# Attention, layer norm and feed-forward on one core: first scores of the next batch, two-part statistics, the last pair's normalisation, the low part of q, and the order of the weight conversions

## The chip, the core and the metric

The kernel runs on one core of a Trainium2 chip. The metric is the device time of one execution in microseconds (us). Five engines work from queues of their own, each in program order: TensorE (PE: matmuls and transposes; PEld: its weight loads), VectorE (DVE), ScalarE (ACT), GpSimd (POOL) and SyncE (SP, which issues the transfers here). A semaphore wait at the head of a queue holds up all that stands behind it.

## The reference

Causal attention over 4 batches, 12 heads, 448 positions and 64 columns a head, in float32; then a layer norm over the 768 columns, a two-layer feed-forward and a residual.

```python
scores = scale * np.matmul(q, k.transpose(0, 1, 3, 2))
scores = np.where(mask, -1000000000.0, scores)
attn = np.exp(scores - np.max(scores, axis=-1, keepdims=True))
attn = attn / (np.sum(attn, axis=-1, keepdims=True) + 1e-09)
x = np.matmul(attn, v)          # heads side by side: (4, 448, 768)
xn = (x - mu) / np.sqrt(var + 1e-06) * g_ln
out = x + np.maximum(xn @ w_ch1, 0.0) @ w_ch2     # 768 -> 3072 -> 768
```

The feed-forward weights come as 64-bit numbers, which the kernel turns into float32 itself.

## The kernel before

**Feed-forward.** All of it is paced by slots, 48 for each batch. A slot is 18 matmuls of 128x448: each float32 operand is a high part and a low part, and high x high, high x low and low x high are added in PSUM. Slots 0 to 11 and 24 to 35 are the first layer (`ph`, L421), the others the second (`po`, L440). `xh`/`xl` are the parts of the normalised input, `hh`/`hl` those of the hidden layer (eviction of `ph` by ACT at L426, then DVE at L427), `wh`/`wl` those of a slot's weights. In batch 0 a slot's weights are converted from the raw 64-bit numbers, four slots ahead: two ACT passes (`convert1`: `w` and `bits`), one on DVE (`convert2`), then ACT writes `wh` (`split1`) and DVE `wl` (`split2`). Later batches read float32 copies back (`full`) and only split them.

**Attention.** Heads go in six pairs (p = 0 to 5) a batch. For a pair: the score matmuls in five groups of row blocks (`SGROUPS`), a DVE pass over each block that masks and finds the row's extreme (L242), the exponential on ACT (`exps`, L256), the division by the row sums (`norm`, L272, on DVE; in batch 0 on POOL for p below `NDVE`), transposes in five groups (`pt`, L288) copied to SBUF as `PT` (L291 on ACT, L293 on DVE), and the product with v (`px`, L303), which ACT copies to `xT` (L307). Batch 0 multiplies in float32. From batch 1 on q and k are split first: ACT writes q's high part `qs`, DVE k's high part `kh`, DVE the low part of q into the other 64 partitions of `qs` (L200), POOL the low part of k, `kl` (L203).

**Layer norm.** `stats` transposes `xT` back (`pln`, L316), up to three column blocks of 128 at a time, and DVE takes the statistics of the piece (`bn_stats`, L319); `aggr` joins them (L326), POOL raises to the power -1/2 (L328), `spread` (PE) puts mean (`mb`) and factor (`rb`) on all partitions, and DVE (`xg`), ACT (`xh`) and POOL (`xl`, L361) write the six blocks.

**Order.** The program is written slot by slot: first what `pre` holds (loads, splits of q and k, exponentials, normalisations, the apply steps of the layer norm), then the weight steps (`ahead`), then the slot's matmuls with their evictions, then `post` (scores, transposes, products with v, statistics). Batch 0's attention lies in the slots below zero, the prologue, with batch 1's first pair begun there; batch b + 1's attention is woven into the feed-forward of batch b, a pair every six slots. PSUM buffers: `sc` 2, `mm` 3 (for `ph`, `po` and in the prologue some scores), `pt` 2 (for transposes and `pln`), `pv` 1 (`px`).

## Time and profile before

| | us |
|---|---|
| three runs | 918.36, 919.53, 921.22 (median 919.53) |
| the profiled execution | 919.61 |
| its span, first to last instruction | 917.8 |
| PE busy in the span | 897.9 (98%) |
| DVE, ACT, POOL busy | 553.8, 452.8, 121.8 |
| mean granted TensorE clock | 0.992 |
| prologue, up to the first feed-forward matmul | 80.04 |
| feed-forward of batches 0, 1, 2, 3 | 221.90, 218.38, 218.41, 179.07 |

What lies around the span is 1.81 us. A timeline row gives start, duration, engine, line, operation, output<-input, shapes and a count; in brackets stands how long the engine stood idle before it and whose end it waited for. A row with a count above 1 joins neighbours of one kind. A row of stretches gives the stretch, its length and then each engine's busy time with its instruction count, the granted clock, the share of the DMA engines and the bytes moved. A matmul's duration includes its pass through the array, so neighbours overlap: the pace is the distance of their starts.

### The profile page before, as it was taken

How to read it: one execution, taken by the hardware profiler on the slowest of the kernel's cores; microseconds unless marked ns; L12 is line 12 of the kernel's file. 1: busy time of each engine (PE TensorE's matmuls, PEld its weight loads, DVE VectorE, ACT ScalarE, POOL GpSimd, SP SyncE). 2: the span in 40 equal slices, each digit the busy share in tenths (PEclk: the TensorE clock that was granted, in tenths of full speed). 3: DMA queues.
4: the chain of work that ended last, by engine and by line, in shares of the span. 5: the costliest groups of instructions: out<-in, count | busy, mean ns of one | idle time of the engine just before them, and what ended most of it. 6: DMA issues, size and time to landing. Idle time of an engine off the chain costs nothing.

```text
span 917.8 us, 12820 instructions
## 1 busy us (share of the span) xinstructions
PE 897.9 (98%) x4864; PEld 790.2 (86%) x4864; DVE 553.8 (60%) x1208; ACT 452.8 (49%) x907; POOL 121.8 (13%) x115
## 2 busy tenths in 40 slices
PE   6988999999999999999999999999999999999998
PEld 4656889888899988988889998888988999999997
DVE  4877788777778566655664676556664634333431
ACT  5955888778865544444442355433542333222320
POOL 5543111101021111100102210011100200000000
PEclk9998999999999999999999999999999999999999
DMA  9920778787778643333313634343222343323210
GB/s 245 338 76 22 287 260 281 282 305 248 254 258 272 232 154 110 109 123 119 103 48 123 214 126 151 120 152 111 84 96 77 120 148 116 120 104 104 103 65 31
DMA packets 35246, 144.36 MB, mean 157 GB/s; under 512 B 4080, under 2 KB 8688, under 8 KB 35184
## 3 DMA queue, kind: packets, MB, share of 16 engines
q1 hardware_dynamic: 35184, 143.54, 45.2%
q8 instruction: 38, 0.62, 0.3%
q14 instruction: 24, 0.20, 0.1%
HBM read 119.15 MB, written 24.38 MB: 156 GB/s over the span
## 4 chain that ended last, share of the span: by engine, by line
PE 88%; ACT 5%; DVE 4%; DMA 1%; issue 1%; SPq 1%; POOL 0%; ACTq 0%
PE po L440 38%; PE ph L421 34%; PE px L303 5%; PE sc L234 4%; PE pt L288 4%; ACT P L256 2%; PE pln L316 1%; DMA raw<-w_dram 1%; PE sc L227 1%; ACT w L99 1%; ACT bits L103 1%; ACT wh L122 1%; DVE P L272 1%; DVE hl L427 1%; DVE wl L126 1%
## 5 line engine op out<-in xcount | busy, mean ns | idle before, releaser
L421 PE MATMUL ph<-xh,wh 128*128 128x448 f32 x576 | 214.5, 372 | 1.4 <-ACT xh L358 1.4
L440 PE MATMUL po<-hh,wh 128*128 128x448 f32 x576 | 214.1, 372 | 0.0
L421 PE MATMUL ph<-xl,wh 128*128 128x448 f32 x576 | 211.7, 368 | 0.5 <-POOL xl L361 0.5
L421 PE MATMUL ph<-xh,wl 128*128 128x448 f32 x576 | 211.3, 367 | 0.2
L440 PE MATMUL po<-hh,wl 128*128 128x448 f32 x576 | 210.7, 366 | 0.0
L440 PE MATMUL po<-hl,wh 128*128 128x448 f32 x576 | 210.6, 366 | 0.0
L427 DVE SCALAR_TENSOR_TENSOR hl<-ph,hh 128x448 fp32r<-128x448 f32 x96 | 59.8, 624 | 145.6 <-ACT hh L426 145.6
L122 ACT ACTIVATE wh<-full 128x768 fp32r<-128x768 f32 x144 | 119.3, 838 | 53.7 <-PE po L440 50.8
L126 DVE TENSOR_TENSOR wl<-full,wh 128x768 fp32r<-128x768 f32 x144 | 136.4, 953 | 0.8 <-ACT wh L122 0.5
L426 ACT ACTIVATE hh<-ph 128x448 fp32r<-128x448 f32 x96 | 52.0, 543 | 153.4 <-PE ph L421 153.2
L256 ACT ACTIVATE P<-P,nm 112x448 f32<-112x448 f32 (+3 forms) x176 | 91.7, 523 | 68.0 <-DVE nm L242 68.0
L421 PEld LDWEIGHTS ph<-xh,wl 128*128 128x128 f32 x576 | 108.6, 189 | 10.6 <-DVE wl L126 2.2
L421 PEld LDWEIGHTS ph<-xh,wh 128*128 128x128 f32 x576 | 108.7, 189 | 10.3 <-ACT xh L358 1.7
L421 PEld LDWEIGHTS ph<-xl,wh 128*128 128x128 f32 x576 | 108.7, 189 | 8.9 <-POOL xl L361 1.0
L440 PEld LDWEIGHTS po<-hh,wl 128*128 128x128 f32 x576 | 108.1, 188 | 9.2 <-DVE wl L126 0.4
L440 PEld LDWEIGHTS po<-hh,wh 128*128 128x128 f32 x576 | 108.2, 188 | 8.5
L440 PEld LDWEIGHTS po<-hl,wh 128*128 128x128 f32 x576 | 108.4, 188 | 8.2
L242 DVE CUSTOM_DVE_ANT_0 P<-sc,mask 112x448 f32<-112x448 f32 (+3 forms) x176 | 70.6, 444 | 51.9 <-PE sc L234 39.6
L203 POOL TENSOR_TENSOR kl<-qkraw,kh 128x896 fp32r<-128x896 f32 x18 | 51.8, 2878 | 377.0 <-DVE kh L193 370.3
L444 DVE TENSOR_TENSOR xT<-po,xT 128x448 f32<-128x448 f32 x48 | 29.9, 623 | 112.7 <-PE po L440 112.7
L288 PE MATMUL pt<-ident,P 112*112 112x112 f32 x440 | 55.1, 262 | 3.8 <-ACT PT L291 2.6
L288 PEld LDWEIGHTS pt<-ident,P 112*112 112x112 f32 x440 | 46.9, 134 | 13.5 <-ACT PT L291 4.1
(63 smaller groups left out, 941.8 us busy)
## 6 DMA issues: line engine op xcount, KB each, us to landing
full<-scratch SPq DMA_DIRECT2D x72, 768.0 KB, 4.2
raw<-w_dram SPq DMA_DIRECT2D x48, 768.0 KB, 5.7
scratch<-w SPq DMA_DIRECT2D x48, 384.0 KB, 2.9
qkraw<-qk_dram SPq DMA_DIRECT2D x18, 896.0 KB, 7.5
out_dram<-xT SPq DMA_DIRECT2D x24, 224.0 KB, 2.0
vt<-v_dram SPq DMA_DIRECT2D x18, 224.0 KB, 5.4
first_qk<-qk_dram SPq DMA_DIRECT2D x8, 224.0 KB, 5.5
rest<-v_dram SPq DMA_DIRECT2D x6, 224.0 KB, 7.8
```

The costliest lines, as they stand in the source:

```text
L122: nc.scalar.activation(out=wh[s], in_=w32[s], func=ACTF.Copy)
L126: nc.vector.tensor_tensor(out=wl[s], in0=w32[s], in1=wh[s].bitcast(F32), op=ALU.subtract)
L203: nc.gpsimd.tensor_tensor(out=kl, in0=rk, in1=kh.bitcast(F32), op=ALU.subtract)
L234: nc.tensor.matmul(pt[:, o:o + n], lhsT=qs[:, h, C * i:C * i + C], rhs=kk[:, h, :n], start=(part == 0), stop=(part == 1),)
L242: nc.vector.tensor_tensor_reduce(out=self.t["P", p, h][:, OFF[i]:OFF[i + 1]], in0=pt[:, o:o + n], in1=mask[:, S - n:], op0=ALU.add, op1=AL ...
L256: nc.scalar.activation(out=pp, in_=pp, func=ACTF.Exp, scale=-1.0, bias=nm[:, x:x + 1], accum_out=self.t["sm", p, h][:, i:i + 1],)
L288: nc.tensor.transpose(pt[:, o:o + C], pp[:, a:a + C], ident[:C, :C])
L303: nc.tensor.matmul(px[D * h:D * h + D, C * j:], lhsT=vt[:, h, j, :], rhs=self.t.pop(("PT", p, h, j)), start=(j == 0), stop=(j == NC - 1),)
L421: nc.tensor.matmul(pm[y], lhsT=w[:, c * P:c * P + P], rhs=z[:, c, :], start=(c == 0 and i == 0), stop=(c == KC - 1 and i == 2),)
L426: nc.scalar.activation(out=hh[:, x + y, :], in_=pm[y], func=ACTF.Relu)
L427: nc.vector.scalar_tensor_tensor(out=hl[:, x + y, :], in0=pm[y], scalar=0.0, in1=hh[:, x + y, :].bitcast(F32), op0=ALU.max, op1=ALU.subtract,)
L440: nc.tensor.matmul(pm, lhsT=w[:, o:o + P], rhs=z[:, x, :], start=(x == 0 and i == 0), stop=(x == HF - 1 and i == 2),)
```

## The change

- **Batch 1's first pair.** Its five score groups stood in the prologue ahead of the products of batch 0's last pair. Now the products of groups 0 and 1 stand behind the last statistics, in `mm` buffers, with their DVE pass (`lows`) behind `aggr` and their exponentials between the `xh` blocks; groups 2 and 3 come after the first feed-forward slot, group 4 after the second. The splits of its q and k come later too (`PARTS`), and all of batch 1's later steps one slot later, its transposes two.
- **Statistics of batch 0** are taken in two parts of three column blocks, not in three of 3, 2 and 1, and the first part starts two slots earlier.
- **`NDVE` 7 to 5:** batch 0's last pair is normalised on DVE.
- **Low part of q** (18 instructions, 64x896): from DVE to POOL, ahead of `kl`.
- **`convert1`** in slots from 0 on is queued behind the slot's evictions and `post` steps, not ahead of them.

```diff
--- before.py
+++ after.py
@@ -29,17 +29,19 @@
 
 SGROUPS = [[(0, 3)], [(0, 0), (0, 2)], [(0, 1), (1, 1)], [(1, 3)], [(1, 0), (1, 2)]]
 TGROUPS = [[(0, 0)], [(0, 1), (0, 3)], [(0, 2), (1, 2)], [(1, 0)], [(1, 1), (1, 3)]]
-HOLE = [-7, 1]
+HOLE = 2
+AHEAD = [-205, -204, -203, -200, -200, -199]
 EARLY = 45
 GAP = 6
 FIRST = -20
+PARTS = [-18, -13]
 SAT0, TAT0, NAT0, END0, EV0 = [-1, 0, 2, 2, 4], [7, 8, 9, 10, 11], [4, 6], 13, [1, 1, 0, 1, 0]
 SAT, TAT, NAT, END, EV = [0, 0, 1, 1, 2], [3, 4, 4, 5, 5], [3, 4], 6, [1, 1, 0, 0, 0]
-EV1 = [1, 1, 1, 1, 1]
-TH0, TH = [38, 40], [18, 30]
+TAT1, END1, EV1 = [4, 5, 5, 6, 6], 7, [1, 1, 1, 1, 1]
+TH0, TH1, TH = [36], [20, 32], [18, 30]
 ELAG = [2, 5, 7]
-NDVE = 7
-STATS = [(0, 3), (3, 5), (5, 6)]
+NDVE = 5
+STATS0, STATS = [(0, 3), (3, 6)], [(0, 3), (3, 5), (5, 6)]
 LAST = 239 / 256
 OFF = [C * (i * (i + 1) // 2) for i in range(NC + 1)]
 
@@ -157,6 +159,7 @@
     class Att:
         def __init__(self, b):
             self.b = b
+            self.spans = STATS if b else STATS0
             self.t = {}
             self.turn = 0
             self.done = set()
@@ -197,19 +200,25 @@
             r = self.t.pop(("raw", p))
             qs, kh, kl = self.t["qk", p]
             rq, rk = r[:, 0:2, :], r[:, 2:4, :]
-            nc.vector.tensor_tensor(
+            nc.gpsimd.tensor_tensor(
                 out=qs[D:], in0=rq[D:], in1=qs[D:].bitcast(F32), op=ALU.subtract
             )
             nc.gpsimd.tensor_tensor(out=kl, in0=rk, in1=kh.bitcast(F32), op=ALU.subtract)
 
         def scores(self, p, grp):
+            self.products(p, grp)
+            self.lows(p, grp)
+
+        def products(self, p, grp):
             if self.b == 0:
                 tag, bufs = (("sc", 2), ("sc", 2), ("mm", 3), ("mm", 3), ("mm", 3))[self.turn % 5]
                 self.turn += 1
+            elif self.b == 1 and p == 0 and grp in SGROUPS[:2]:
+                tag, bufs = "mm", 3
             else:
                 tag, bufs = "sc", 2
             pt = ps.tile([C, S], F32, tag=tag, name="sc", bufs=bufs)
-            nm = sb.tile([C, 2], F32, tag="nm", name="nm", bufs=8)
+            self.t["sc", p, tuple(grp)] = pt
             o = 0
             for h, i in grp:
                 n = C * (i + 1)
@@ -236,6 +245,10 @@
                             start=(part == 0), stop=(part == 1),
                         )
                 o += n
+
+        def lows(self, p, grp):
+            pt = self.t.pop(("sc", p, tuple(grp)))
+            nm = sb.tile([C, 2], F32, tag="nm", name="nm", bufs=8)
             o = 0
             for x, (h, i) in enumerate(grp):
                 n = C * (i + 1)
@@ -308,7 +321,7 @@
             self.done.add(("pv", p))
 
         def stats(self, part, x):
-            c0, c1 = STATS[part]
+            c0, c1 = self.spans[part]
             assert all(("pv", c) in self.done for c in range(c0, c1))
             self.done.add(("stats", part, x))
             pt = ps.tile([C, S], F32, tag="pt", name="pln")
@@ -321,9 +334,10 @@
         def aggr(self):
             mv = sb.tile([C, NC, 2], F32, tag="mv", name="mv", bufs=2)
             ve = sb.tile([C, NC], F32, tag="ve", name="ve", bufs=2)
-            assert all(("stats", i, x) in self.done for i in range(3) for x in range(NC))
+            n = len(self.spans)
+            assert all(("stats", i, x) in self.done for i in range(n) for x in range(NC))
             for x in range(NC):
-                nc.vector.bn_aggr(out=mv[:, x, :], in_=self.stat[:, x])
+                nc.vector.bn_aggr(out=mv[:, x, :], in_=self.stat[:, x, :n])
             nc.vector.tensor_scalar_add(ve, mv[:, :, 1], 1e-6)
             nc.gpsimd.tensor_tensor(out=ve, in0=ve, in1=mhalf, op=ALU.pow)
             self.t["mv"], self.t["ve"] = mv, ve
@@ -374,7 +388,9 @@
             if self.b == 0:
                 sat, tat, nat, end, ev = SAT0, TAT0, NAT0, END0, EV0
             else:
-                sat, tat, nat, end, ev = SAT, TAT, NAT, END, EV1 if self.b == 1 else EV
+                sat, tat, nat, end, ev = SAT, TAT, NAT, END, EV
+            if self.b == 1:
+                tat, end, ev = TAT1, END1, EV1
             period = 6
             for p in range(NP):
                 t0 = period * p
@@ -388,14 +404,24 @@
                 for x, grp in enumerate(TGROUPS):
                     put(post, t0 + tat[x], self.transposes, p, grp, "act" if ev[x] else "dve")
                 for x, grp in enumerate(SGROUPS):
+                    if self.b == 1 and p == 0:
+                        if x < 2:
+                            put(post, AHEAD[0], self.products, p, grp)
+                            put(post, AHEAD[1], self.lows, p, grp)
+                            put(pre, AHEAD[2], self.exps, p, grp)
+                        else:
+                            put(post, AHEAD[x + 1], self.scores, p, grp)
+                            put(pre, AHEAD[x + 1] + 1, self.exps, p, grp)
+                        continue
                     put(post, t0 + sat[x], self.scores, p, grp)
                     put(pre, t0 + sat[x] + 1, self.exps, p, grp)
             tl = period * (NP - 1) + end + 1
-            th = TH0 if self.b == 0 else TH
+            th = TH0 if self.b == 0 else TH1 if self.b == 1 else TH
             for x in range(NC):
                 put(post, th[0] + x, self.stats, 0, x)
-                put(post, th[1] + x, self.stats, 1, x)
-                put(post, tl + x // 2, self.stats, 2, x)
+                if self.b:
+                    put(post, th[1] + x, self.stats, 1, x)
+                put(post, tl + x // 2, self.stats, len(self.spans) - 1, x)
             ta = tl + NC // 2
             put(pre, ta, self.aggr)
             put(post, ta, self.spread)
@@ -461,14 +487,16 @@
             def slot(t):
                 if b != 1:
                     return t + shift
+                if t <= -100:
+                    return t + 200
                 if t < 0:
-                    return t + FIRST
-                return t - 2 + HOLE[0] if t <= 2 else t - 3 + HOLE[1]
+                    return PARTS[t + 2] if t >= -2 else t + FIRST
+                return t - 3 + HOLE
 
             for mine, whole in ((first, pre), (second, post)):
                 for t, fs in mine.items():
                     whole.setdefault(slot(t), []).extend(fs)
-            return slot(min(min(first), min(second)))
+            return min(map(slot, [*first, *second]))
 
         start = add_batch(0)
         for p in range(NP):
@@ -493,7 +521,8 @@
             for f, args in pre.get(s, []):
                 f(*args)
             for f, x in ahead.get(s, []):
-                f(x)
+                if s < 0 or f is not convert1:
+                    f(x)
             if s >= 0:
                 if s == 0:
                     hh = sb.tile([P, HF, S], F32R, tag="hh", name="hh")
@@ -503,6 +532,9 @@
                 next(feed)
             for f, args in post.get(s, []):
                 f(*args)
+            for f, x in ahead.get(s, []):
+                if s >= 0 and f is convert1:
+                    f(x)
         for _ in feed:
             pass
 
```

(Line numbers of the changed kernel are 3 to 26 higher than before.) On PE, the end of the prologue before, from the last transposes of batch 0 to the scores of batch 1's first pair (two pieces: behind the products of pair 4, then around those of pair 5):

```order
L288 MATMUL pt<-ident,P 112x112 x8
L316 MATMUL pln<-ident,xT 112x128 x3
L288 MATMUL pt<-ident,P 112x112 x4
L316 MATMUL pln<-ident,xT 112x128 x3
L288 MATMUL pt<-ident,P 112x112 x4
L316 MATMUL pln<-ident,xT 112x128 x5
L288 MATMUL pt<-ident,P 112x112 x4
L316 MATMUL pln<-ident,xT 112x128 x5
L234 MATMUL sc<-kh,qs 112x448
```

```order
L234 MATMUL sc<-kh,qs 112x448
L234 MATMUL sc<-kl,qs 112x448
L303 MATMUL px<-PT,rest 64x448 x2
L303 MATMUL px<-PT,rest 64x336 x2
L303 MATMUL px<-PT,rest 64x224 x2
L303 MATMUL px<-PT,rest 64x112 x2
L316 MATMUL pln<-ident,xT 112x128 x2
L234 MATMUL sc<-kh,qs 112x112
```

And with the change, from the last transposes on:

```order
L301 MATMUL pt<-ident,P 112x112 x4
L329 MATMUL pln<-ident,xT 112x128 x3
L301 MATMUL pt<-ident,P 112x112 x4
L329 MATMUL pln<-ident,xT 112x128 x3
L301 MATMUL pt<-ident,P 112x112 x4
L329 MATMUL pln<-ident,xT 112x128 x3
L301 MATMUL pt<-ident,P 112x112 x8
L316 MATMUL px<-PT,rest 64x448 x2
L316 MATMUL px<-PT,rest 64x336 x2
L316 MATMUL px<-PT,rest 64x224 x2
L316 MATMUL px<-PT,rest 64x112 x2
L329 MATMUL pln<-ident,xT 112x128 x12
```

```order
L243 MATMUL sc<-kh,qs 112x448
L243 MATMUL sc<-kl,qs 112x448
L243 MATMUL sc<-kh,qs 112x112
L243 MATMUL sc<-kl,qs 112x112
L243 MATMUL sc<-kh,qs 112x336
L243 MATMUL sc<-kl,qs 112x336
L350 MATMUL mb<-ident,mv 128x112 x4
L355 MATMUL rb<-ident,ve 128x112 x4
```

The scores (`sc<-kh,qs`) left the place ahead of the last `px`; the six matmuls of groups 0 and 1 stand behind the statistics now, and the others come behind the first 18 `ph`. The pieces of statistics have one size.

On POOL, the prologue's last normalisations and the split of batch 1's first pair, before and with the change (with what each waits for):

```order
L272 TENSOR_SCALAR rest<-rest,r 112x336
L203 TENSOR_TENSOR kl<-qkraw,kh 128x896 [waits DMAHW6_49,DVE_49]
L272 TENSOR_SCALAR rest<-rest,r 112x112 [waits DVE_49,Activation_49]
L272 TENSOR_SCALAR rest<-rest,r 112x224 [waits PE_49]
L272 TENSOR_SCALAR rest<-rest,r 112x448 [waits PE_49]
L272 TENSOR_SCALAR rest<-rest,r 112x336 [waits Activation_49]
L272 TENSOR_SCALAR P<-P,r 112x112 [waits PE_49,DVE_49,Activation_49,Pool_49]
```

```order
L285 TENSOR_SCALAR rest<-rest,r 112x112 [waits DVE_49,Activation_49]
L285 TENSOR_SCALAR rest<-rest,r 112x224 [waits PE_49]
L285 TENSOR_SCALAR rest<-rest,r 112x448 [waits PE_49]
L285 TENSOR_SCALAR rest<-rest,r 112x336 [waits Activation_49]
L203 TENSOR_TENSOR qs<-qkraw,qs 64x896 [waits DMAHW6_49,Activation_49,Pool_49]
L206 TENSOR_TENSOR kl<-qkraw,kh 128x896 [waits DVE_49,Pool_49]
L342 TENSOR_TENSOR ve<-ve,mhalf 112x4 [waits DVE_49]
```

`kl` moved behind the normalisations of pair 4, with the low part of q ahead of it; the eight instructions for pair 5 are gone from POOL. `kl` now waits for POOL's own semaphore too, which is the end of the instruction ahead of it.

On DVE, before and with the change, from the copy of pair 4's third transposes to that of its fifth, which the products of pair 4 wait for (`P,nm` is the pass over a score block of pair 5, the `nm` row behind it reads the extreme out):

```order
L293 COPY PT<-pt 112x448
L267 TENSOR_SCALAR r<-sm 112x4
L268 RECIPROCAL r<-r 112x4
L242 ISA P,nm<-sc,mask 112x112
L242 ISA nm 112x1
L242 ISA P,nm<-sc,mask 112x336
L242 ISA nm 112x1
L293 COPY PT<-pt 112x448
```

```order
L306 COPY PT<-pt 112x448
L280 TENSOR_SCALAR r<-sm 112x4
L281 RECIPROCAL r<-r 112x4
L285 TENSOR_SCALAR P<-P,r 112x112
L285 TENSOR_SCALAR P<-P,r 112x224
L285 TENSOR_SCALAR P<-P,r 112x448
L285 TENSOR_SCALAR P<-P,r 112x336
L255 ISA P,nm<-sc,mask 112x112
L255 ISA nm 112x1
L255 ISA P,nm<-sc,mask 112x336
L255 ISA nm 112x1
L306 COPY PT<-pt 112x448
```

With the change the normalisation of pair 5's first head stands between the two copies; it was on POOL.

## Rows read from the trace of the kernel before

**Rows 1.** Stretches: span; PE PEld DVE ACT POOL busy; clock, DMA, GB/s.

```profile
0.00:80.04 80.04, 64.79 (x369) 42.64 (x369) 51.54 (x179) 51.88 (x147) 37.29 (x71) 0.94 0.61 189
80.04:301.94 221.90, 220.74 (x1201) 194.22 (x1201) 171.62 (x325) 167.82 (x296) 35.53 (x19) 0.99 0.75 262
301.94:520.32 218.38, 218.38 (x1217) 195.62 (x1216) 134.02 (x311) 92.83 (x199) 26.42 (x14) 1.00 0.35 126
738.73:917.80 179.07, 175.55 (x865) 162.05 (x863) 63.83 (x84) 48.27 (x69) 0.00 (x0) 1.00 0.28 98
```

**Rows 2.** Timeline near 47 us: start, us, engine, line, op, xcount [idle before].

```profile
45.98 2.14 POOL L272 TENSOR_SCALAR rest<-rest,r 112x112 f32<-112x112 f32 x4 [2.09 <-DVE r L268]
48.08 2.08 POOL L203 TENSOR_TENSOR kl<-qkraw,kh 128x896 fp32r<-128x896 f32 x1
47.09 4.02 DVE L200 TENSOR_TENSOR qs<-qkraw,qs 64x896 fp32r<-64x896 f32 x1
51.82 0.78 PE L303 MATMUL px<-PT,rest 112*64 112x336 f32 x5 [2.42 <-DVE PT L293]
```

**Rows 3.** Timeline: two heads normalised on POOL, one on DVE.

```profile
58.96 3.82 POOL L272 TENSOR_SCALAR P<-P,r 112x112 f32<-112x112 f32 x8 [3.61 <-DVE r L268]
117.77 1.19 DVE L272 TENSOR_SCALAR P<-P,r 112x112 f32<-112x112 f32 x4
```

**Rows 4.** Timeline of PE from pair 4's products to pair 5's.

```profile
59.12 2.37 PE L303 MATMUL px<-PT,rest 112*64 112x448 f32 x16
...
63.08 0.59 PE L288 MATMUL pt<-ident,P 112*112 112x112 f32 x4
...
67.62 0.45 PE L234 MATMUL sc<-kh,qs 128*112 128x448 f32 x1
...
70.32 2.11 PE L303 MATMUL px<-PT,rest 112*64 112x448 f32 x16
```

**Rows 5.** Statistics by form: ns min, median, max; the three shapes.

```profile
L319 DVE BATCH_NORM_STATS2 stat<-pln x48: 279/426/566, 63.2 to 708.5; 112x6 f32<-112x384 f32 x16, 112x6 f32<-112x256 f32 x16, 112x6 f32<-112x128 f32 x16
```

**Rows 6.** Timeline of PE at the layer norm.

```profile
76.96 1.69 PE L341 MATMUL rb<-ident,ve 112*128 112x112 f32 x8 [0.46 <-POOL ve L328]
80.04 0.74 PE L421 MATMUL ph<-xh,wh 128*128 128x448 f32 x1 [1.38 <-ACT xh L358]
```

**Rows 7.** POOL memsets by form: busy us, mean ns.

```profile
L171 POOL MEMSET first_qk<- 64x448 f32 x4 | 1.9, 466 | 0.4 <-POOLq L530 0.3
L480 POOL MEMSET mask<- 112x448 f32 x1 | 0.5, 476 | 0.0
```

**Rows 8.** Timeline near 86 us: POOL, DVE.

```profile
85.05 1.18 POOL L361 TENSOR_TENSOR xl<-xg,xh 128x448 fp32r<-128x448 f32 x1
86.30 1.18 POOL L361 TENSOR_TENSOR xl<-xg,xh 128x448 fp32r<-128x448 f32 x1
85.53 0.73 DVE L267 TENSOR_SCALAR r<-sm 112x4 f32<-112x4 f32 x1
```

**Rows 9.** Waits in batch 0's feed-forward: us, times, longest.

```profile
DVE hl L427 <- ACT hh L426: 24.6, 16, 3.5
PEld ph L421 <- DVE wl L126: 2.2, 6, 0.5
```

**Rows 10.** Timeline near 125 us: POOL, DVE.

```profile
123.76 3.60 POOL L203 TENSOR_TENSOR kl<-qkraw,kh 128x896 fp32r<-128x896 f32 x1 [26.88 <-DVE kh L193]
125.91 2.40 DVE L200 TENSOR_TENSOR qs<-qkraw,qs 64x896 fp32r<-64x896 f32 x1
128.32 0.96 DVE L126 TENSOR_TENSOR wl<-w,wh 128x768 fp32r<-128x768 f32 x1
```

**Rows 11.** Timeline in batch 1's feed-forward: DVE, PE.

```profile
358.09 0.96 DVE L126 TENSOR_TENSOR wl<-full,wh 128x768 fp32r<-128x768 f32 x1
360.50 0.37 PE L440 MATMUL po<-hh,wl 128*128 128x448 f32 x1
```

**Rows 12.** Stretch as in rows 1, from the first feed-forward matmul.

```profile
80.04:90.00 9.96, 9.46 (x38) 8.21 (x39) 9.08 (x16) 6.67 (x13) 7.05 (x6) 0.79 0.00 0
```

## The prediction

> **What bounds the kernel now.** I read the stretches first, batch by batch [rows 1]. From 301.94 us on PE is busy for the whole stretch (218.38 of 218.38): nothing that the change does on other engines can shorten it, only lengthen it. Two stretches have room: the prologue, where PE works 64.79 of 80.04 us, and batch 0's feed-forward, which carries the same work as batch 1's and takes 221.90 us, 3.5 more. Each must be read for what PE waits for. In the prologue that is a chain over all engines, with one event that stands out [rows 2]: the low part of q, one DVE instruction, takes 4.02 us from 47.09, ends 0.95 after POOL's `kl`, and PE's products of a pair then start 2.42 late. In batch 0's feed-forward it is the low part of the weights: PE's weight loads wait six times, 2.2 us in all, for `wl` [rows 9].
>
> The profiled execution took 919.61 us (span 917.8 and 1.81 around it), 0.1 above the median of 919.53; the sum is made against 919.61. About 0.3% (2.8 us) is what a measurement of this kernel can tell from no change.
>
> **The change part by part.**
>
> *The splits of batch 1's first pair.* The DVE instruction of 4.02 us goes, and with its neighbours to a later place; `kh` and the high part of q only move within engines that are idle a third of this stretch (DVE 51.54, ACT 51.88 of 80.04), so I cost their moving at nothing. Without that cover each would add its own length to the chain, under 1 us. On DVE, ahead of the copy that pair 4's products wait for, the normalisation of pair 5's first head comes in, four instructions, 1.19 [rows 3]. POOL's low part of q will then be running when that normalisation asks; I let it wait 0.1. Saved: 4.02 - 1.19 - 0.1 = 2.7. The bounds are 0 (if ACT's exponentials and copies were the later ones anyhow) and 4.0; PE's own 2.42 of waiting behind the stall is near the value taken.
>
> How long POOL takes for it no row shows. POOL's `kl`, 128x896 of the same operation, takes 2.08 [rows 2], and a memset on 64 partitions takes as long as one on 112 (466 and 476 ns) [rows 7], so time goes with columns: 2.08. The bounds are 1.04 (half the partitions, half the time) and 2.8 (halfway to the 3.60 that `kl` takes where DVE is in its way [rows 10]).
>
> *From pair 4's products to pair 5's.* Now the end of the first is 61.49 (59.12 + 2.37), and PE comes to the scores at 67.62: eleven pieces of transposes in 6.13 us, 0.56 a piece, each waiting for a buffer to be copied out. The scores with one piece of statistics take 67.62 to 70.32, 2.70 us, then pair 5's products begin [rows 4]. With the change no scores stand here, and the pieces are eight: five of transposes, three of statistics (one went ahead of pair 4's products, the rest behind pair 5's). From start to start 11.20 becomes 2.37 + 8 x 0.56 + 0.5 = 7.4, where 0.5 stands for the second head's normalisation on DVE between its other copies. Normalising two heads took POOL 3.82 [rows 3]; DVE needs 2.4, so these transposes find their operands earlier than now. Saved: 3.8; bounds 0.8 (each of the eight pieces 0.37 slower, behind DVE) and 4.3 (nothing for the normalisation).
>
> *Layer norm.* Behind the last products there are now twelve transposes in four pieces with statistics over 384 columns, 0.56 each, where there were four over 128 columns, 0.28 each (the ends of the range in [rows 5]), and a piece over 256 columns, 0.43, that stood ahead of them: 4 x 0.28 - 0.43 = +0.7. The six matmuls of scores fill the time in which PE waits for `aggr`; their DVE passes stand behind `ve`, where DVE waits for `rb` while PE needs 1.69 for that [rows 6]; three exponentials stand between `xh` blocks, for which ACT has room as long as DVE sets the pace. All of this at nothing; if it isn't covered, +1.0. The feed-forward would then begin at 80.04 - 2.7 - 3.8 + 0.7 = 74.2.
>
> *Batch 0's feed-forward.* Ten score matmuls come in, as many columns as six matmuls of 448. The last batch's stretch holds 864 matmuls in 179.07 us, 0.207 each [rows 1]: +1.2. What is taken away is waiting. Today, around each of pairs 1 to 5, DVE and POOL stand in each other's way [rows 10]: `kl` takes 3.60, of which the last 2.08, from 125.28, are its own; DVE's low part of q asks at 125.91, takes 2.40 and ends 0.95 behind it; `wl` comes after that and ends at 129.28. With both low parts on POOL, the one for q would run 125.28 to 127.36, `wl` 127.36 to 128.32, a full 0.96 earlier, and `kl` after it, to 129.44. Behind `kl` on POOL stands nothing until the next pair or the layer norm, and only the pair's scores, some slots on, wait for it. And `hl` waited 24.6 us for `hh` [rows 9], which stood on ACT behind the conversions; now `hh` goes first, so DVE comes to its weight steps sooner. The conversions themselves are late by that eviction, but they are four slots ahead. Saved: 1.9 of the 2.2 us; bounds 0 and 2.2. Net -0.7.
>
> *Batches 2 and 3's attention.* The `wl` behind such a pair of instructions ends at 359.05, and PE asks at 360.50, 1.45 later [rows 11]. Nothing to gain, and nothing to lose until it comes 1.45 later. Batch 1's steps one slot later shift work inside a busy stretch: 0.
>
> Sum: -2.7 - 3.8 + 0.7 + 1.2 - 1.9 = -6.5, so 919.6 - 6.5 = **913.1 us**.
>
> **A rule against the rows.** The sum has DVE wait for one POOL instruction at a time. That is what [rows 8] show: DVE asked at 85.53 while POOL's `xl` ran until 86.23, and was done at 86.26, before the next `xl` began at 86.30, which had something of its own to wait for. But [rows 2] show another thing: from 47.09 on DVE waited through the two last of POOL's normalisations, which began without a gap, and through all of `kl`. `kl` will wait for the end of the low part of q, a gap like that at 86.23; if the gap is not enough, the next case comes about.
> The Trainium skill (SBUF — State Buffer, "SBUF: two separate sides") says that VectorE and GpSimd share a pair of ports under an exclusive lock, which an instruction holds to its end while the other is fully blocked. By that rule alone DVE waits for the low part of q and no more, 913.1; the trace agrees on the blocking, and [rows 2] show a wait longer than one instruction, by which it would be 920.3.
>
> **The rivals.**
>
> *POOL keeps the way through both.* For: [rows 2]. DVE's first normalisation then waits 2.08 longer, and the first term shrinks to 0.6; the feed-forward begins 3.7 earlier, not 5.8. In batch 0's feed-forward both low parts run 125.28 to 129.44 before `wl`, which ends at 130.40, 1.1 later than today; five times, with about half of it covered, 3.0 us more of waiting instead of 1.9 less. Sum: -0.6 - 3.8 + 0.7 + 1.2 + 3.0 = +0.5, so 920.1: no change. In batches 1 and 2's stretches 1.1 is within the 1.45. Against: [rows 8].
>
> *The chain in the prologue is held by others.* Where ACT's exponentials or copies end as late as DVE's, half of the first two terms stays: -3.3 + 0.7 - 0.7 = -3.3, 916.3. For: ACT is as busy as DVE there (51.88 and 51.54). Against: PE's wait names the DVE copy [rows 2].
>
> *Slower: POOL becomes the bound in every stretch.* If POOL keeps the way through both and needs 2.8 for the low part of q, `wl` comes 1.1 + 0.7 = 1.8 later than today; it decides from the point where this passes the 1.45 that PE has left [rows 11]. Then some eleven pairs of batches 2 and 3 lose 0.35 each, and five in batch 0's feed-forward 0.7 more: 920.1 + 3.9 + 3.5 = 927.5. For: POOL's time in the stretches that were full is then on the path. Against: [rows 7] speak for 2.08.
>
> *Better: the feed-forward begins at full clock.* Its first matmul took 0.74 [rows 6], at 1.2 GHz, after a pause; the granted clock was 0.79 over the first 9.96 us [rows 12], which is 2.1 us of full clock. With scores in the pause, some of it may stay: -1.5, 911.6.
>
> **How the numbers follow.** Forecast 45%, POOL keeps the way 25%, chain held by others 13%, slower 9%, better 8%. The forecast's own range is 911 to 915.5, from the bounds of its terms. The whole range reaches from 909.5 (the better case with the ends of the first two terms) to 920.8, which holds the second case; what is slower stays out, with a tail below. Faster by over 0.3% means under 916.8: forecast and better nearly whole, half of the third case, 60%; within 0.3%, the second case and the other half, 28%; slower 12%.
>
> **What would show it.** Right: no DVE instruction over 2 us near 47; pair 4's products start near 56.4, pair 5's near 64; the feed-forward near 74.2; the weight loads' waits for `wl` in batch 0's feed-forward under 0.5; POOL's low part of q near 2.08, and DVE instructions starting between it and `kl`; later stretches at 218.4. Wrong: DVE instructions that end only with `kl`; waits of PE for `wl` above 2.2 us or in the stretches from 301.94 on; a low part of q well over 2.1; a layer norm longer by more than 1.2.

## The result and the profile after

The changed kernel takes 926.33 us (median of five runs, 924.5 to 927.29) against 921.0 (five runs, 918.36 to 921.88): ratio 1.0067, 95% interval 1.0049 to 1.0084 (the two medians alone give 1.0058). It is slower by 0.6 to 0.7%, where 913.1 was forecast. The profiled execution took 927.29 us, span 925.5, against 919.61 and 917.8 before.

The stretches of the kernel after, cut as in [rows 1] (stretch, length, busy time of PE, PEld, DVE, ACT and POOL, clock, DMA share, GB/s):

```profile
0.00:76.64 76.64, 61.63 (x359) 40.81 (x359) 50.18 (x172) 48.77 (x135) 35.79 (x64) 0.96 0.64 198
76.64:300.81 224.17, 221.37 (x1210) 195.44 (x1211) 175.07 (x330) 170.55 (x308) 51.57 (x25) 0.99 0.74 260
300.81:523.57 222.76, 220.19 (x1218) 195.29 (x1216) 138.36 (x305) 92.78 (x198) 37.26 (x19) 1.00 0.34 123
746.29:925.50 179.21, 175.56 (x865) 162.07 (x863) 63.84 (x84) 48.26 (x69) 0.00 (x0) 1.00 0.28 97
```

The prologue is 3.4 us shorter. Batch 0's feed-forward is 2.3 longer, and batch 1's, which had been full (218.38 busy of 218.38), is 4.4 longer and has 2.57 us in which PE is idle; batch 2's went the same way, 218.41 to 222.72 (746.29 - 523.57). -3.4 + 2.3 + 4.4 + 4.3 + 0.1 = +7.7, the whole difference of the two executions.

What PE waits for in other engines in batch 1's stretch now (waits of PE and of its weight loads: us, times, longest); before, it waited for none of these there:

```profile
PEld ph L447 <- DVE wl L128: 2.8, 3, 1.0
PE ph L447 <- DVE wl L128: 1.7, 3, 0.6
PEld po L466 <- DVE wl L128: 1.0, 1, 1.0
PEld pt L301 <- DVE P L285: 0.9, 3, 0.3
PE po L466 <- DVE wl L128: 0.6, 1, 0.6
```

Four late `wl`, and late normalisations (`P`) ahead of transposes. One of the four, first in the kernel before (timeline of POOL, DVE, PEld and PE; `kl`, the normalisation of one head, `kh`, `wl`, and the weight load and matmul that need it):

```profile
354.41 2.72 POOL L203 TENSOR_TENSOR kl<-qkraw,kh 128x896 fp32r<-128x896 f32 x1 [25.64 <-DVE kh L193]
352.55 1.19 DVE L272 TENSOR_SCALAR P<-P,r 112x112 f32<-112x112 f32 x4
353.65 0.62 DVE L193 CAST kh<-qkraw 128x896 fp32r<-128x896 f32 x1
354.19 0.95 DVE L126 TENSOR_TENSOR wl<-full,wh 128x768 fp32r<-128x768 f32 x1
355.86 0.19 PEld L440 LDWEIGHTS po<-hh,wl 128*128 128x128 f32 x1
356.06 0.36 PE L440 MATMUL po<-hh,wl 128*128 128x448 f32 x1
```

and the same place after (timeline of ACT, POOL, DVE, PE):

```profile
351.90 0.96 ACT L195 ACTIVATE qs<-qkraw 128x896 fp32r<-128x896 f32 x1
353.00 2.13 POOL L203 TENSOR_TENSOR qs<-qkraw,qs 64x896 fp32r<-64x896 f32 x1 [23.44 <-ACT qs L195]
356.36 2.70 POOL L206 TENSOR_TENSOR kl<-qkraw,kh 128x896 fp32r<-128x896 f32 x1 [1.24 <-DVE kh L196]
352.57 3.11 DVE L285 TENSOR_SCALAR P<-P,r 112x112 f32<-112x112 f32 x4
355.60 0.62 DVE L196 CAST kh<-qkraw 128x896 fp32r<-128x896 f32 x1
356.13 0.95 DVE L128 TENSOR_TENSOR wl<-full,wh 128x768 fp32r<-128x768 f32 x1
357.00 0.61 DVE L453 SCALAR_TENSOR_TENSOR hl<-ph,hh 128x448 fp32r<-128x448 f32 x1
358.07 1.81 DVE L128 TENSOR_TENSOR wl<-full,wh 128x768 fp32r<-128x768 f32 x1
357.14 0.47 PE L466 MATMUL po<-hh,wl 128*128 128x448 f32 x1 [0.58 <-DVE wl L128]
```

The reader is to follow POOL first. Its low part of q waits for ACT's high part alone. That ends at 352.86, and POOL starts at 353.00, while DVE is in the middle of normalising a head: the four instructions take 3.11 instead of 1.19. `kh` and `wl` behind them come 1.94 later (354.19 to 356.13). PE had 0.92 to spare at this `wl` (355.14 to the matmul at 356.06; to its weight load, which waits for `wl` too, 0.72); now it waits. `kl`, which needs `kh`, starts at 356.36 and holds DVE a second time, at the next `wl` (1.81 instead of 0.96), whose slack of 1.45 [rows 11] is enough. `hl` (0.61), which reads PSUM beside one SBUF tensor, ran during `kl` unhindered.

One pair of the same stretch shows the opposite case. There the low part of q came after the normalisation and `kh`; the normalisation took its 1.19 and no matmul was late:

```profile
380.41 1.19 DVE L285 TENSOR_SCALAR P<-P,r 112x112 f32<-112x112 f32 x4
381.52 0.62 DVE L196 CAST kh<-qkraw 128x896 fp32r<-128x896 f32 x1
382.50 2.49 POOL L203 TENSOR_TENSOR qs<-qkraw,qs 64x896 fp32r<-64x896 f32 x1 [23.44 <-ACT qs L195]
```

In the prologue, POOL and DVE at batch 1's first pair, and PE at pair 4's products, then at the start of pair 5's and of the feed-forward:

```profile
53.24 2.09 POOL L203 TENSOR_TENSOR qs<-qkraw,qs 64x896 fp32r<-64x896 f32 x1 [0.98 <-DVE nm L255]
55.41 2.08 POOL L206 TENSOR_TENSOR kl<-qkraw,kh 128x896 fp32r<-128x896 f32 x1
54.03 1.32 DVE L280 TENSOR_SCALAR r<-sm 112x4 f32<-112x4 f32 x1
55.39 0.18 DVE L281 RECIPROCAL r<-r 112x4 f32<-112x4 f32 x1
55.61 2.87 DVE L285 TENSOR_SCALAR P<-P,r 112x112 f32<-112x112 f32 x4
59.69 1.66 PE L316 MATMUL px<-PT,rest 112*64 112x336 f32 x10 [2.10 <-DVE PT L306]
...
66.88 0.59 PE L316 MATMUL px<-PT,rest 112*64 112x448 f32 x1
...
76.64 0.47 PE L447 MATMUL ph<-xh,wh 128*128 128x448 f32 x1 [1.38 <-ACT xh L372]
```

The stall of 4.02 at 47 us [rows 2] is gone, and another has come in its place: the sum of four columns (L280, 1.32) waits for the low part of q, slips in between the two POOL instructions, and the normalisation behind it then waits for `kl` (2.87 for what takes 1.19). PE waits 2.10 for the copy behind that, nearly the 2.42 of before. Before, the wait lay within pair 3's products; now those run through, and it lies within pair 4's.

### The profile page after: what moved, and what is told of

The parts are those of the page before. It is cut to its first block, busy times and chain, and to the rows that moved or that the text cites. A ratio compares the mean times of both kernels' runs of the same rounds, so it can differ in the third digit from the quotient of the medians.

```text
span 925.5 us, 12882 instructions
## 1 busy us (share of the span) xinstructions
PE 898.9 (97%) x4864; PEld 788.9 (85%) x4864; DVE 565.7 (61%) x1194; ACT 452.3 (49%) x907; POOL 159.7 (17%) x125
## 4 chain that ended last, share of the span: by engine, by line
PE 86%; DVE 10%; ACT 1%; issue 1%; DMA 1%; SPq 1%; POOL 0%; DVEq 0%; ACTq 0%
PE ph L447 36%; PE po L466 33%; PE px L316 5%; PE sc L243 4%; PE pt L301 4%; DVE P L285 3%; DVE wl L128 2%; PE sc L236 2%; DVE w L112 1%; DMA raw<-w_dram 1%; PE pln L329 1%; DVE kh L196 1%; ACT hh L452 0%; PE rb L355 0%; DVE hl L453 0%
## 5 line engine op out<-in xcount | busy, mean ns | idle before, releaser
L128 DVE TENSOR_TENSOR wl<-full,wh 128x768 fp32r<-128x768 f32 x144 | 147.1, 1028 | 0.5 <-ACT wh L124 0.5
L203 POOL TENSOR_TENSOR qs<-qkraw,qs 64x896 fp32r<-64x896 f32 x18 | 45.9, 2553 | 336.1 <-ACT qs L195 334.7
L285 DVE TENSOR_SCALAR P<-P,r 112x112 f32<-112x112 f32 (+3 forms) x152 | 65.9, 497 | 1.4
L112 DVE SCALAR_TENSOR_TENSOR w<-w,bits 128x768 uint32<-128x768 uint32 x48 | 56.4, 1174 | 9.0 <-ACT bits L105 9.0
```

The source lines that it names most:

```text
L112: nc.vector.scalar_tensor_tensor(out=w, in0=w, scalar=3, in1=bits.pop(s), op0=ALU.logical_shift_left, op1=ALU.bitwise_or,)
L128: nc.vector.tensor_tensor(out=wl[s], in0=w32[s], in1=wh[s].bitcast(F32), op=ALU.subtract)
L203: nc.gpsimd.tensor_tensor(out=qs[D:], in0=rq[D:], in1=qs[D:].bitcast(F32), op=ALU.subtract)
L285: eng.tensor_scalar(out=pp, in0=pp, scalar1=r[:, i:i + 1], scalar2=1.0, op0=ALU.mult, op1=ALU.mult,)
```

## The experiments

Prologues are compared from the start of pair 2's products (39.68 before, 40.20 after; the third start of `px` on PE) on: two executions with the same program up to the feed-forward (the kernel before and the fourth experiment) reached that point at 39.68 and 37.69, with a granted clock of 0.86 and 1.00 between 20 and 30 us, and from there took 40.36 and 39.58. Column by column these two have 21.81 and 20.66, 8.83 both, 9.72 and 10.09, so a difference of 1 us in the first column, or of 0.4 in the third, is not to be told from chance. The times of this table come from the timeline of PE, in us, one execution of each kernel; a ratio is to runs of the kernel before that were taken beside it.

| kernel | pair 2's start to pair 4's end | to pair 5's start | to the feed-forward | batch 0's stretch | batch 1's | ratio to before |
|---|---|---|---|---|---|---|
| before | 21.81 | 8.83 | 9.72 | 221.90 | 218.38 | |
| after | 21.14 | 5.54 | 9.76 | 224.18 | 222.75 | 1.0067 |
| 1 q on VectorE | 18.15 | 5.46 | 9.70 | 224.60 | 218.38 | 0.9944 |
| 2 q on GpSimd alone | 19.82 | 8.83 | 10.09 | 227.25 | 222.76 | 1.0146 |
| 3 kl first | 19.82 | 5.06 | 9.63 | 222.43 | 218.37 | 0.9949 |
| 4 conversions behind alone | 20.66 | 8.83 | 10.09 | 219.53 | 218.41 | 0.9975 |
| 5 kl first, last pair on GpSimd | 17.94 | 4.73 | 9.82 | 222.33 | 218.38 | 0.9918 |
| 6 kl first, scores before the pause | 21.42 | 7.81 | 10.82 | 221.67 | 218.37 | 0.9961 |
| 7 kl first, three parts | 19.83 | 6.74 | 8.75 | 221.66 | 218.38 | 0.9943 |
| 8 q's high part later | 18.00 | 7.41 | 10.97 | 222.31 | 218.38 | 0.9938 |
| 9 q on VectorE, last pair on GpSimd | 17.95 | 7.86 | 10.48 | 223.57 | 218.37 | 0.9969 |
| 10 old prologue, kl first | 21.18 | 8.83 | 10.09 | 220.32 | 218.39 | 0.9967 |

**1. The low part of q on VectorE again.**

```diff
-            nc.gpsimd.tensor_tensor(
+            nc.vector.tensor_tensor(
                 out=qs[D:], in0=rq[D:], in1=qs[D:].bitcast(F32), op=ALU.subtract
```

> The changed kernel with one line undone: the low part of q on VectorE again. Theory 1 (POOL's low part of q, which starts as soon as ScalarE's high part is there, holds VectorE up in the middle of a normalisation, and kl then holds it up a second time): the stretches of batches 1 and 2 fall from 222.7 back to 218.4 us each, the prologue from 76.6 to about 75.4, batch 0's feed-forward from 224.2 to about 222.5; about 915 us. Rival (the loss lies in batch 1's later steps or in the conversions behind the evictions): the later stretches stay at 222.7 and the time near 926.

Measured 913.38 us, 0.9944 (0.9922 to 0.9966). Its stretch for batch 1 is full again:

```profile
295.81:514.19 218.38, 218.38 (x1217) 195.62 (x1216) 133.79 (x311) 92.78 (x198) 25.26 (x13) 1.00 0.36 125
```

One line decides whether the change is a loss or a gain. The prologue is shorter than expected: 33.31 from pair 2's products on, 3.1 less than after. Batch 0's stretch stayed long (224.60 against about 222.5 expected).

**2. That line alone, in the kernel before.** The same edit turned round, in the kernel before.

> The kernel before with this one line of the change: the low part of q on GpSimd ahead of kl. Theory 1: the stretches of batches 1 and 2 grow from 218.4 to 222.7 us each, batch 0's by 2 to 3, the prologue by 0 to 2; about 931 us. Rival (the loss comes only together with the other parts): within 2 us of the kernel before.

Measured 931.74 us, 1.0146 (1.012 to 1.0172): the stretches of batches 1 and 2 are 222.76 and 222.70, as after. The loss belongs to this line and to nothing that goes with it. It costs batch 0's stretch 5.4, more than expected, and the prologue from pair 2 on is 1.6 shorter, where 0 to 2 longer was expected.

**3. `kl` first.**

```diff
+            nc.gpsimd.tensor_tensor(out=kl, in0=rk, in1=kh.bitcast(F32), op=ALU.subtract)
             nc.gpsimd.tensor_tensor(
                 out=qs[D:], in0=rq[D:], in1=qs[D:].bitcast(F32), op=ALU.subtract
             )
-            nc.gpsimd.tensor_tensor(out=kl, in0=rk, in1=kh.bitcast(F32), op=ALU.subtract)
```

> The changed kernel with kl ahead of the low part of q on GpSimd: the same work there, but it begins only when VectorE has written kh, and both run one behind the other. Theory 1 (the place ahead of kh makes two holds, the first in a normalisation): one hold of about 4.2 us, which wl reaches with its slack of 1.45; stretches of batches 1 and 2 at 218.4 to 219, about 916 us. Rival (the sum of GpSimd's busy time is what VectorE loses, wherever it lies): 222 or more, about 926.

Measured 913.44 us, 0.9949 (0.9933 to 0.9966), batch 1's stretch 218.37. GpSimd does as much as after, and PE loses nothing: not the amount of its work costs time, but when the first of the two begins. `kl` is released by DVE's own `kh`, and in batch 1's stretch the `wl` with the small slack is already running when `kl` starts; it takes its usual 0.95:

```profile
346.81 0.62 DVE L196 CAST kh<-qkraw 128x896 fp32r<-128x896 f32 x1
347.35 0.95 DVE L128 TENSOR_TENSOR wl<-full,wh 128x768 fp32r<-128x768 f32 x1
347.66 2.62 POOL L203 TENSOR_TENSOR kl<-qkraw,kh 128x896 fp32r<-128x896 f32 x1 [22.95 <-DVE kh L196]
```

Timeline of POOL and DVE in batch 0's feed-forward, the place that answers to [rows 10]:

```profile
119.96 3.51 POOL L203 TENSOR_TENSOR kl<-qkraw,kh 128x896 fp32r<-128x896 f32 x1 [22.32 <-ACT wh L124]
123.55 2.71 POOL L204 TENSOR_TENSOR qs<-qkraw,qs 64x896 fp32r<-64x896 f32 x1
121.91 2.37 DVE L128 TENSOR_TENSOR wl<-w,wh 128x768 fp32r<-128x768 f32 x1
124.21 2.86 DVE L112 SCALAR_TENSOR_TENSOR w<-w,bits 128x768 uint32<-128x768 uint32 x1
127.00 0.61 DVE L453 SCALAR_TENSOR_TENSOR hl<-ph,hh 128x448 fp32r<-128x448 f32 x1
```

`kl` ends at 123.47, `wl` 0.81 later, and the low part of q, which stretches to 2.71 from 2.09, behind it: DVE gets its turn between two POOL instructions of which the second waits for the first. The one hold of about 4.2 that was expected did not come.

**4. Conversions behind the evictions, alone, in the kernel before.** The edits of the last two pieces of the diff.

> The kernel before with convert1 behind a slot's evictions and post steps, and nothing else. If the hidden layer's eviction was held up by the conversions and this reached PE: batch 0's feed-forward 221.9 to about 220.5 us, about 918. If VectorE's low parts alone set wl: no change within 0.5 us. If the later conversions make wl later: longer by up to 2.

Measured 916.18 us, 0.9975 (0.9961 to 0.9988). Batch 0's stretch is 219.53, 2.4 shorter; no weight load in it waits for `wl` until the last slots (0.4 at 282 us, against 2.6 in all before), and `hl` waits less for `hh` than the 24.6 of [rows 9]:

```profile
DVE hl L427 <- ACT hh L426: 16.4, 15, 1.7
```

So the hidden layer's eviction did reach PE.

**5. The last pair's normalisation on GpSimd, in 3.** (Run twice.)

```diff
-NDVE = 5
+NDVE = 7
```

> kl first, and batch 0's last pair normalised on GpSimd again. If the two normalisations on VectorE cost the chain more ahead of pair 4's products than they give back ahead of pair 5's: pair 4's products end 1 to 1.2 us earlier and pair 5's start no later, about 912.5 us. If GpSimd's 3.8 us for them is the longer way, with the low parts of q and k ahead of it now: pair 4's products to pair 5's longer by 2 to 4 us, about 916.

> kl first with the last pair on GpSimd once more, beside the two others on one chip: about 912, from pair 2's products to the feed-forward 32.5 us.

Measured 912.1 us, 0.9918 (0.9896 to 0.9941), and 911.9, 0.9916 (0.9899 to 0.9933); from pair 2's products on 32.49 and 32.50 us. Pair 4's products end 1.9 earlier than in 3 and pair 5's start no later. In the prologue this part of the change is a loss of 2.0 (34.51 to 32.49). Without it and with `kl` first the kernel beats the one before and the changed one; against 3 the intervals of the ratios still meet.

**6. The scores ahead of the last products, in 3.**

```diff
-AHEAD = [-205, -204, -203, -200, -200, -199]
+AHEAD = [-209, -209, -208, -208, -208, -207]
-PARTS = [-18, -13]
+PARTS = [-22, -21]
-            elif self.b == 1 and p == 0 and grp in SGROUPS[:2]:
+            elif False:
```

> kl first, and all five score groups of batch 1's first pair ahead of and around pair 5's products again, its splits at their old places; the rest as changed. If the scores moved out were on the chain: prologue 2.5 to 3 us longer (pair 4's products to pair 5's 5.1 to about 7.2 us, pair 5's to the feed-forward 0.5 longer), batch 0's feed-forward 1.2 shorter; about 915 us. If the chain of copies sets the pace there anyway: prologue unchanged, about 912.

Measured 915.83 us, 0.9961 (0.9948 to 0.9975). The prologue from pair 2 on is 40.05 against 34.51 in 3: 2.8 between pair 4's and pair 5's products, 1.2 behind them, and 1.6 ahead. The last is not the scores': there the two subtractions (45.90 to 51.01) stand in front of pair 4's normalisations on GpSimd, and the granted clock was 0.61 between 52 and 56 us. Batch 0's stretch is 0.8 shorter. With 2.8 + 1.2 - 0.8 = 3.2, moving the scores is the largest of the gains that these experiments tell apart.

**7. Statistics in three parts, in 3.**

```diff
-STATS0, STATS = [(0, 3), (3, 6)], [(0, 3), (3, 5), (5, 6)]
+STATS0, STATS = [(0, 3), (3, 5), (5, 6)], [(0, 3), (3, 5), (5, 6)]
-TH0, TH1, TH = [36], [20, 32], [18, 30]
+TH0, TH1, TH = [36, 40], [20, 32], [18, 30]
-                if self.b:
-                    put(post, th[1] + x, self.stats, 1, x)
+                put(post, th[1] + x, self.stats, 1, x)
```

> kl first, and batch 0's statistics in three parts again (3, 2 and 1 column blocks), the first part still two slots early. If the forecast of the layer norm was right (two parts cost 0.7 behind the last products, and save transposes ahead of them): pair 5's products start 1 us later and the feed-forward comes 0.7 less behind them; within 0.5 us of kl first. If two parts cost nothing behind: 1 us longer.

Measured 914.41 us, 0.9943 (0.9924 to 0.9962), not to be told from 3 by time. In the timeline pair 5's products start 1.7 later and the feed-forward follows 0.9 sooner (8.75 for 9.63). Two parts are worth 0.8 in the prologue; batch 0's stretch is 0.8 shorter with three, so nothing of it is left in the time.

**8. The high part of q later, in the changed kernel.** The line `nc.scalar.activation(out=qs, in_=rq, func=ACTF.Copy)` moves from `split1` to the head of `split2`.

> The changed kernel with ScalarE's high part of q one slot later, directly ahead of GpSimd's low part; GpSimd's order (low part of q, then kl) stays. Theory 1 (it is the early start, ahead of kh and in a normalisation, that makes two holds): stretches of batches 1 and 2 at 218.4 to 219.5 us, about 914 to 916. Rival (the order, low part of q ahead of kl, with a gap between): they stay above 221, about 922 or more.

Measured 914.07 us, 0.9938 (0.9913 to 0.9962); the stretches of batches 1 and 2 are 218.38 and 218.41:

```profile
296.36:514.74 218.38, 218.38 (x1218) 195.62 (x1216) 127.73 (x305) 92.83 (x198) 35.58 (x19) 1.00 0.37 125
```

The order on GpSimd is that of the changed kernel; only the start of its first instruction moved, past the normalisation, `kh` and the `wl` with the small slack. In batch 1's stretch:

```profile
346.96 1.19 DVE L285 TENSOR_SCALAR P<-P,r 112x112 f32<-112x112 f32 x4
348.61 0.95 DVE L128 TENSOR_TENSOR wl<-full,wh 128x768 fp32r<-128x768 f32 x1
351.44 2.63 POOL L203 TENSOR_TENSOR qs<-qkraw,qs 64x896 fp32r<-64x896 f32 x1 [23.52 <-ACT qs L202]
```

That alone removes the loss.

**9. The low part of q on VectorE and the last pair on GpSimd, in the changed kernel.** The edits of 1 and 5.

> The changed kernel with the low part of q on VectorE and the last pair's normalisation on GpSimd, both as before; the other parts as changed. If the two moves between VectorE and GpSimd were the whole of the loss: from pair 2's products to the feed-forward 32 to 33 us, stretches of batches 1 and 2 at 218.4, about 911. If the prologue needs GpSimd free of the normalisations: 34 or more, about 914.

Measured 916.2 us, 0.9969 (0.9955 to 0.9983), with 36.29 from pair 2's products on: the second way. DVE's low part of q stands here for 4.62 us behind POOL's normalisations and `kl`, as it did at 47 us before, only later and between the statistics:

```profile
54.22 1.92 POOL L285 TENSOR_SCALAR P<-P,r 112x112 f32<-112x112 f32 x4 [0.55 <-DVE r L281]
56.10 2.08 POOL L206 TENSOR_TENSOR kl<-qkraw,kh 128x896 fp32r<-128x896 f32 x1
54.51 4.62 DVE L203 TENSOR_TENSOR qs<-qkraw,qs 64x896 fp32r<-64x896 f32 x1
```

So in this order of work, normalising the last pair on GpSimd pays only where the low part of q is there too.

**10. The old prologue with `kl` first.** The edits of 4 and 3 in the kernel before.

> The kernel before with two parts of the change alone: conversions behind the evictions, and the low part of q on GpSimd but behind kl. If scores in the pause and statistics in two parts carry the gain in the prologue (3.3 us of it between pair 4's and pair 5's products): prologue only 1 to 2 us shorter than before, batch 0's feed-forward 219.5 to 220.5, about 915. If the one hold of VectorE near 47 us was most of it: about 912.

Measured 916.65 us, 0.9967 (0.9956 to 0.9978). The prologue gains nothing that shows (40.10 against 40.36 and 39.58), though no DVE instruction stands for 4 us any more (the longest near that place is 1.05): both subtractions now stand in front of pair 4's normalisations on GpSimd, 47.98 to 53.10, so pair 4's products wait where pair 3's had waited. It doesn't tell what the hold alone was worth. Batch 0's stretch keeps most of experiment 4's gain.

## Why the prediction was wrong

**The step that failed** is "Nothing to gain, and nothing to lose until it comes 1.45 later", with the assumption under it that POOL's low part of q would run where `kl`'s own part had run (125.28 to 127.36). I placed it by its queue, ahead of `kl`, and forgot that it doesn't wait for `kh`: it started when ACT's high part was there, 1.4 us before `kl` had started (353.00 against 354.41), in a normalisation. So the slack that counted was not the 1.45 of the `wl` behind `kl` but the 0.92 of the one ahead of it, and the delay was 1.94. In batch 1's stretch four of six pairs lose about 0.85 by it (0.74 at the matmul and 0.1 at the next) and the transposes wait 0.9 in all: 4 x 0.85 + 0.9 = 4.3 a stretch. That is shown from three sides: put back, the loss goes (1); alone, it comes (2); and with the same work later it goes as well (3, 8). The direction of the slower rival was the true one, at another price: the low part of q takes 2.09 alone, as forecast, and the limit was passed by where it stands and not by being slow. That its 927.5 lies beside the measured 927.29 is luck: it has 3.9 for batches 1 and 2's stretches, where 8.7 were lost, from an instruction of 2.8, and makes up the rest elsewhere.

**Point by point, against the profile of before.** The splits and pair 4's products, forecast -2.7, measured -0.7 (21.81 to 21.14; the granted clock was 0.83 between 50 and 60 us before, and 1.00 after). A second step failed here, the 0.1 of waiting for the normalisation: it waited 1.68 (2.87 for 1.19), and the sum ahead of it took 1.32 where it takes 0.16 when nothing holds it. With the low part of q on DVE (1) this piece took 18.15, so the rival with the chain held by others does not fit. Here the rival with POOL keeping the way through both came to the measured number (-0.6), which is partly luck, since one program gave 21.81 and 20.66 here, and its mechanism is only partly right: the pause between the two POOL instructions did let DVE in, as [rows 8] said, but for one instruction, and that was the sum of four columns.

Pair 4's to pair 5's products: forecast -3.8, measured -3.3 from the end of the one to the start of the other; from start to start, as the forecast counts, 11.20 became 10.82 and not 7.4, mostly because the wait of 2.10 lies within pair 4's products.

The layer norm: +0.7, measured 0.0; experiment 7 gives 0.9 for the statistics alone, so the forecast's cost was there; experiment 6 gives 1.2 saved by the scores that no longer stand behind pair 5's products, which I had put at nothing.

Batch 0's feed-forward: -0.7, measured +2.3. There the conversions' order gives 2.4 (experiment 4) where I had 1.9 for all that is taken away. The place of the low part of q costs 1.8 (224.18 against 222.43 in experiment 3; 5.4 in the kernel before, experiment 2), and the moved scores 0.8 (3 against 6) where I had 1.2. Batch 1's later steps, which I had put at 0, cost about 1.3: experiments 6 and 10 begin the stretch at much the same clock (0.70 and 0.68 over 10 us) and take 221.67 and 220.32, and in every kernel with these steps the weight loads of this stretch wait 1.0 us for ACT's copies ahead of `pln`, in none without. These two differ in the prologue as well, so this is a reading and no test. The better case came in small part: the first matmul took 0.47 and not 0.74, and the clock over the first 10 us was 0.83 for 0.79.

Batches 1 and 2: 0, measured +8.7. One figure of the prediction doesn't come out of its working: the 920.3 beside the ports is 920.1 by the sum of its second case.

**The rule on the ports.** The Trainium skill (SBUF — State Buffer, "SBUF: two separate sides") has the lock held for one whole instruction, the other engine blocked. The trace agrees: the low part of q held the normalisation until its end, 355.13, and experiment 3 shows DVE getting in after one. The 4.62 of experiment 9, like the 4.02 of [rows 2], is longer than one instruction, so the rule alone doesn't say whose turn comes next. The mistake was not in the rule but in the place where the lock is taken.

Batch 0's stretch differs by up to 2.3 us between experiments 1, 3, 5 and 8. Experiment 9 tells the two parts apart: from the feed-forward on it is the program of 1, with the same waits for `wl` (2.8 us of the weight loads), but its granted clock over the first 10 us was 0.83 against 0.66, and it took 1.0 less (223.57 against 224.60). Experiment 5 had the clock of 9 and 1.4 of waits for `wl`, and took 1.2 less again (222.33). What stays open is which of batch 1's later steps costs the 1.3.

## What to carry to other kernels

An instruction moved to an idle engine starts when its own inputs are there, not where its neighbour in the queue used to start: look up what releases it, and what the engines it shares a way with are doing at that moment. Take the slack from the next consumer behind that moment, at each of the places where it repeats. And a bundle of edits with one bad line hides its good ones: here a loss of 8.7 us in two stretches covered a gain that is 0.8% with two lines changed.

## What the runs showed of the hardware

- The four-column sum on DVE (L280) took 1.32 beside POOL's low part of q, and the normalisation, with one large SBUF input, was held like those with two: 3.11 for 1.19. `hl` (0.61 at 357.00), which reads PSUM, took no longer beside POOL.
- A held DVE instruction gets its turn between two POOL instructions of which the second waits for the first (experiment 3, 0.81 after the end of `kl`); through POOL instructions without such a wait it waited for all (4.02 in [rows 2], 4.62 in experiment 9).
- The low part of q on 64 partitions took POOL 2.09, `kl` on 128 partitions 2.08: here the columns and not the partitions set the time, as with the memsets [rows 7].
- The same program reached pair 2's products 2.0 us apart in two executions, with a granted clock of 0.86 and 1.00 between 20 and 30 us. That is as much as some parts of the change are worth, so parts were compared from a common point.
